# One PSUM tile for each bank in a fused attention and MoE kernel

## The chip, the cores and the metric

The kernel runs on one core of one Trainium2 chip. Its time is the device time of one execution in microseconds; the time shown for a version is the median of several runs. Engines: TensorE (PE, with weight loads as PEld), VectorE (DVE), ScalarE (ACT), GpSimd (POOL) and SyncE (SP), which issues the DMAs. PSUM is the memory that matmuls write: eight banks, each of 512 float32 in each of 128 partitions.

## The reference

```python
def reference(**kwargs):
    ...
    attn_out = _attn_ref(**attn_kwargs)       # q, k, v: 8 x 8 x 576 x 64, softmax in chunks of 64 rows
    B, H, S, D = attn_out.shape
    x = np.ascontiguousarray(attn_out.transpose(0, 2, 1, 3)).reshape(B * S, H * D)   # 4608 x 512
    x = _moe_ref(x=x, **moe_kwargs)           # a = x @ w1; b = x @ w2; ((a * b) @ w3) @ w_out
    return _moe2_ref(x=x, **moe2_kwargs)      # h = x @ w_in; (h * cos(h)) @ w_out
```

w1 and w2 are 512 x 1024, w3 is 1024 x 1024, the first w_out 1024 x 512; w_in is 512 x 2048, the second w_out 2048 x 512. The weights come as 64-bit floats.

## The kernel before

A product of float32 quality is made of float16 halves: each operand is split into a high and a low part, and three matmuls (high x high, high x low, low x high) add up in one bank. That is why matmuls come in threes of lines (L831 to L833, L891 to L893, L1171 to L1173).

The 4608 tokens are nine blocks of 512. The work has these stages:

- Weights (0 to about 200 us, and pieces later): 64-bit words are turned into float32 by DVE, ACT and POOL; w3 and w_out are multiplied into one matrix on PE (`w3_row`: transposes L792, matmuls L800, copies L429).
- Attention (`attention`), 36 tiles of 128 tokens, up to about 760 us: q and k are transposed (L600) into a bank of ps_t and copied (L429); scores (L615) go into a pair of banks; DVE L626 and L629 read the pair; the probabilities are transposed (L649) and copied; the products with v (L664) go into a pair again, which ACT L676 and DVE L679 read.
- `ab`: per block, a and b for eight slices, twelve matmuls each (L831 to L833) into one bank; ACT L857 evicts a, DVE L860 evicts b and multiplies.
- `u_of`: per block four products of 24 matmuls (L891 to L893), evicted by L433 or L435, with scales that pass through small matmuls in ps_t (`all_max`: L461, L469).
- `h_of` and `y_of` (from about 805 us): h is made by seven products (a Strassen form) of six matmuls of 256 columns each (L1101), 42 matmuls a step and eight steps a block, into four banks x, y, z and w; ACT L1116 and DVE L1110 evict them. Then h * cos(h) on ACT, DVE and POOL (L1135 to L1157). y takes 48 matmuls a tile in four pieces of twelve (L1171 to L1173); ACT L1178 evicts a tile, SP L1181 stores it. y of one block runs between steps of h of the next; after the last h only y is left.

The order of the work is not written out by hand. Every step is put down as an operation (`Plan.op`) with its engine, an assumed cost, a due time and the buffers that it reads and writes. `Plan.order` (L110) plays the operations through in assumed time, gives each buffer a place in its pool, and `emit` (L227) writes the instructions in the order found. In each engine's queue the instructions then run in this order. Semaphore waits are not put down by the kernel: the tile framework finds them from the accesses of the instructions to tiles, in the order in which they were written out.

PSUM is four tiles of two banks each (L319, L320): ps_s is banks 0 and 1, ps_t 2 and 3, ps_m 4 and 5, ps_n 6 and 7. The pools hand out banks or pairs of these (L328 to L334):

```python
ps_t = bank_pool(2, 3)                              # transposes, small matmuls
ps_s = pair_pool(0)                                 # attention
ps_s0 = pair_pool(0, 4)                             # attention of the first two blocks
ps_mm = bank_pool(4, 5, 6, 7)                       # w3, ab from block 1 on, u
ps_mm0 = bank_pool(6, 7)                            # ab of block 0
ps_h = bank_pool(0, 1, 2, 3, 4, 5, queue=True)      # h
ps_y = bank_pool(6, 7)                              # y
```

Of the kernel before, what the change touches and what calls it, by code (L numbers as in the profile page):

```python
# [11 lines left out]
F32 = mybir.dt.float32  # L12
# [7 lines left out]
P = 128  # L20
# [13 lines left out]
class Buf:  # L34
# [8 lines left out]

    @property
    def ap(self):
        return self.pool.aps[self.place]


class Pool:
# [11 lines left out]
class Plan:  # L61
# [162 lines left out]
                done += 1  # L224
        return order

    def emit(self):  # L227
        order = self.order()
        for o in order:
            o.fn(o.eng) if o.many else o.fn()  # L230
        return order


PLANS = []
# [3 lines left out]
def fused_kernel(  # L238
# [41 lines left out]
    psum = ctx.enter_context(tc.tile_pool(name="psum", bufs=1, space=bass.MemoryType.PSUM))  # L280
    u_dram = dram.tile([NB, P, KD, T], F32, name="u_dram")

    plan = Plan()
# [23 lines left out]
    def plain(ap):  # L307
        return ap

    def halves_of(ap):  # L310
        return ap.bitcast(F16).rearrange("p (k s e) -> p k s e", s=2, e=512)

    def one_half(ap):
        return ap.bitcast(F16).rearrange("p (s e) -> p s e", s=2)
# [1 line left out]
    def words(ap):  # L316
        return ap.bitcast(U32).rearrange("p (n w) -> p n w", w=2)

    banks = psum.tile([P, 2, 512], F32, name="ps_s"), psum.tile([P, 2, 512], F32, name="ps_t")  # L319
    banks += psum.tile([P, 2, 512], F32, name="ps_m"), psum.tile([P, 2, 512], F32, name="ps_n")  # L320

    def bank_pool(*ix, queue=False):
        return Pool([("PS", i, 1) for i in ix], [banks[i // 2][:, i % 2] for i in ix], queue)

    def pair_pool(*ix):
        return Pool([("PS", i, 2) for i in ix], [banks[i // 2] for i in ix])

    ps_t = bank_pool(2, 3)  # L328
    ps_s = pair_pool(0)
    ps_s0 = pair_pool(0, 4)  # L330
    ps_mm = bank_pool(4, 5, 6, 7)
    ps_mm0 = bank_pool(6, 7)
    ps_h = bank_pool(0, 1, 2, 3, 4, 5, queue=True)
    ps_y = bank_pool(6, 7)  # L334
# [6 lines left out]
        queue=True,  # L341
# [58 lines left out]
    pair = 42 * MM / 2  # L400
# [8 lines left out]
    with tc.manual_schedule():  # L409
# [750 lines left out]
        def y_of(bl):  # L1160
            tg, wout = gh[bl], wpart[1]
            last = bl == NB - 1
            prio = start_h[bl] + (8 * pair + 20.0 if bl == 0 else period) + Y0
            for j in range(TPB):
                ps = Buf(ps_y, f"psy{bl}_{j}")
                for pc in range(4):
                    pr = prio + (pc * 4 + j if last else j * 4 + pc) * 24 * MM
                    def f(ps=ps, j=j, pc=pc):
                        js = slice(j * P, (j + 1) * P)
                        for kk in range(4 * pc, 4 * pc + 4):  # L1170
                            nc.tensor.matmul(ps.ap, tg.ap[:, kk, 0, js], wout.ap[:, kk, 0], start=(kk == 0), stop=False)  # L1171
                            nc.tensor.matmul(ps.ap, tg.ap[:, kk, 0, js], wout.ap[:, kk, 1], start=False, stop=False)  # L1172
                            nc.tensor.matmul(ps.ap, tg.ap[:, kk, 1, js], wout.ap[:, kk, 0], start=False, stop=(kk == K2 - 1))  # L1173
                    ks = range(4 * pc, 4 * pc + 4)
                    op("PE", 12 * MM, pr, f, r=[(tg, (s, kk)) for s in range(2) for kk in ks] + [(wout, kk) for kk in ks], w=[ps])
                yo, iy = Buf(yo_p, f"yo{bl}_{j}"), hsc[bl]
                def f(ps=ps, yo=yo, iy=iy):
                    nc.scalar.activation(yo.ap, ps.ap, AF.Copy, scale=iy[1])  # L1178
                op("ACT", 0.69, pr, f, r=[ps, iy[0]], w=[yo])
                def f(yo=yo, j=j):  # L1180
                    nc.sync.dma_start(out[bl * T + j * P : bl * T + (j + 1) * P, :], yo.ap)  # L1181
                op("SP", 0.6, pr, f, r=[yo], size=P * 2 * KB)
# [28 lines left out]
        for bl in range(NB):  # L1211
# [3 lines left out]
            u_load(bl, start_h[bl] - 12.0)  # L1215
            h_of(bl)
            y_of(bl)
        PLANS.append(plan.emit())


# [28 lines left out]
```

## Time and profile before

| what | value |
|---|---|
| median of 3 runs | 1561.65 us (1561.44 to 1567.07) |
| the profiled execution | 1563.77 us, span 1561.9 us |
| PE busy | 1480.4 us (95%) |
| DVE busy | 1073.8 us (69%) |
| ACT busy | 743.5 us (48%) |
| POOL busy | 376.6 us (24%) |
| mean granted TensorE clock | 0.985 |

Busy is the time in which an engine has an instruction running. A row of a wait names the engine and line that stood idle and, behind the arrow, the tile and line of the instruction that ended the wait. A tile's name covers both of its banks. Matmuls overlap: the next one starts before the last one has ended.

### The profile page before, as it was taken

The numbers are of one execution on the slowest core, as the hardware profiler recorded it, in microseconds if no ns is written. First come the engines' busy times: TensorE is split into PE (matmuls) and PEld (weight loads), VectorE is DVE, ScalarE is ACT, GpSimd is POOL, SyncE is SP. The second block draws the span as 40 slices with busy tenths as digits, with TensorE's granted clock in tenths as the row PEclk, the third lists the DMA queues.
The fourth block names the chain that finished last, engine by engine and source line by source line (L and its number), as shares of the span: only waits on it lengthen the run. The fifth ranks groups of instructions, "written<-read, shape, count | busy, mean of one in ns | idle before, by whom it ended". The sixth has DMA issues, their size and how long they took to land.

```text
span 1561.9 us, 26229 instructions
## 1 busy us (share of the span) xinstructions
PE 1480.4 (95%) x10424; PEld 861.1 (55%) x10424; DVE 1073.8 (69%) x2007; ACT 743.5 (48%) x1206; POOL 376.6 (24%) x295
## 2 busy tenths in 40 slices
PE   6887899999999999999999899999999999999998
PEld 4443444545455545455457566666666666666643
DVE  7867788788664647865458787767777777767610
ACT  5654352465422214512127675656565656556520
POOL 2333224043300101200013343322223222322200
PEclk7999999999999999999999999999999999999999
DMA  9873476757131317380400000010101010100000
GB/s 279 229 182 92 115 256 202 214 170 218 54 89 28 82 28 192 119 264 8 155 35 14 35 15 35 14 41 14 41 15 41 14 42 14 41 14 14 14 21 27
DMA packets 155259, 135.93 MB, mean 87 GB/s; under 512 B 118144, under 2 KB 118144, under 8 KB 153984
## 3 DMA queue, kind: packets, MB, share of 16 engines
q1 hardware_dynamic: 155136, 134.25, 29.0%
q8 instruction: 82, 1.34, 0.4%
q14 instruction: 41, 0.34, 0.1%
HBM read 103.81 MB, written 30.41 MB: 86 GB/s over the span
## 4 chain that ended last, share of the span: by engine, by line
PE 89%; DVE 5%; ACT 4%; issue 1%; DMA 1%; ACTq 0%; SPq 0%; DVEq 0%
PE ps_n L1171 8%; PE ps_n L1172 8%; PE ps_n L1173 8%; PE ps_t L1101 7%; PE ps_s L1101 7%; PE ps_m L1101 7%; PE ps_n L831 4%; PE ps_n L833 4%; PE ps_n L832 4%; PE ps_m L831 4%; PE ps_m L833 4%; PE ps_m L832 4%; PE ps_n L800 3%; PE ps_n L891 2%; PE ps_n L893 2%; PE ps_n L892 2%
## 5 line engine op out<-in xcount | busy, mean ns | idle before, releaser
L1101 PEld LDWEIGHTS <-WIN 128*128 128x128 f16 x3024 | 295.8, 98 | 62.4 <-issue 14.3
L1151 POOL TENSOR_TENSOR WG<-WG,TMP 128x512 f32<-128x512 f32 x119 | 158.8, 1344 | 448.8 <-ACT TMP L1148 428.1
L1101 PE MATMUL ps_t<-XHL,WIN 128*128 128x256 f16 x1032 | 127.2, 273 | 4.2 <-DVE WG L1110 2.5
L1101 PE MATMUL ps_s<-XHL,WIN 128*128 128x256 f16 x1002 | 124.2, 273 | 5.4 <-DVE WG L1110 4.2
L1171 PE MATMUL ps_n<-ATT,W 128*128 128x512 f16 x320 | 122.0, 381 | 4.0 <-ACT TMP L1178 3.2
L831 PE MATMUL ps_n<-XHL,W 128*128 128x512 f16 x308 | 117.3, 381 | 8.8 <-ACT TMP L857 5.8
L1101 PE MATMUL ps_m<-XHL,WIN 128*128 128x256 f16 x990 | 122.9, 273 | 2.1 <-DVE WG L1110 2.0
L1172 PE MATMUL ps_n<-ATT,W 128*128 128x512 f16 x320 | 122.0, 381 | 0.0
L1173 PE MATMUL ps_n<-ATT,W 128*128 128x512 f16 x320 | 121.9, 381 | 0.0
L832 PE MATMUL ps_n<-XHL,W 128*128 128x512 f16 x308 | 117.2, 381 | 0.0
L833 PE MATMUL ps_n<-XHL,W 128*128 128x512 f16 x308 | 117.0, 380 | 0.0
L1135 ACT ACTIVATE TMP<-WG,magic 128x512 f32<-128x512 f32 x144 | 98.9, 711 | 32.3 <-DVE WG L1110 31.8
L1148 ACT ACTIVATE TMP<-TMP,half_pi 128x512 f32<-128x512 f32 x144 | 102.4, 719 | 20.0 <-DVE TMP L1145 17.5
L1139 DVE SCALAR_TENSOR_TENSOR TMP<-TMP,WG 128x512 f32<-128x512 f32 x144 | 106.1, 761 | 1.0 <-ACT TMP L1135 1.0
L831 PE MATMUL ps_m<-XHL,W 128*128 128x512 f16 x268 | 101.6, 379 | 2.5 <-ACT TMP L857 2.5
L644 POOL TENSOR_TENSOR ATT<-ATT,SMALL 128x512 f32<-128x512 f32 x31 | 34.1, 1101 | 287.0 <-DVE SMALL L641 193.7
L833 PE MATMUL ps_m<-XHL,W 128*128 128x512 f16 x268 | 101.6, 379 | 0.0
L832 PE MATMUL ps_m<-XHL,W 128*128 128x512 f16 x268 | 101.6, 379 | 0.0
L1171 PE MATMUL ps_n<-ATT,WG 128*128 128x512 f16 x256 | 97.0, 379 | 2.3 <-ACT TMP L1178 2.3
L832 PEld LDWEIGHTS <-W 128*128 128x128 f16 x576 | 56.4, 98 | 74.0 <-issue 12.4
L1173 PE MATMUL ps_n<-ATT,WG 128*128 128x512 f16 x256 | 97.0, 379 | 0.0
L1172 PE MATMUL ps_n<-ATT,WG 128*128 128x512 f16 x256 | 97.0, 379 | 0.0
(167 smaller groups left out, 2891.9 us busy)
## 6 DMA issues: line engine op xcount, KB each, us to landing
WIN<-in_moe_w_out_dram SPq DMA_DIRECT2D x40, 512.0 KB, 5.1
WIN<-in_moe_w_in_dram SPq DMA_DIRECT2D x32, 512.0 KB, 6.0
ATT<-in_v_dram SPq DMA_DIRECT2D x144, 64.0 KB, 2.5
u_dram<-TMP SPq DMA_DIRECT2D x36, 256.0 KB, 3.6
ATT<-u_dram SPq DMA_DIRECT2D x9, 1024.0 KB, 4.8
out_dram<-TMP SPq DMA_DIRECT2D x36, 256.0 KB, 2.0
ATT<-in_q_dram SPq DMA_DIRECT2D x32, 256.0 KB, 3.8
ATT<-in_k_dram SPq DMA_DIRECT2D x32, 256.0 KB, 4.3
```

Of the source, the lines that this page charges most:

```text
L800: nc.tensor.matmul(acc.ap, wT.ap[:, x * P : (x + 1) * P], wof.ap[:, 0, 4 * g + x], start=(g == 0 and x == 0), stop=(g == 1 and x == 3),)
L831: nc.tensor.matmul(ps, left(kk, 0), right(kk, 0), start=(kk == 0), stop=False)
L832: nc.tensor.matmul(ps, left(kk, 0), right(kk, 1), start=False, stop=False)
L833: nc.tensor.matmul(ps, left(kk, 1), right(kk, 0), start=False, stop=(kk == n - 1))
L1101: nc.tensor.matmul(ps.ap[:, side * half : (side + 1) * half], win.ap[:, b, k, g, w_, fs], t.ap[:, a, k, u_], start=(k == 0 and m == 0), st ...
L1135: nc.scalar.activation(r.ap, hs(), AF.Identity, bias=magic)
L1139: nc.vector.scalar_tensor_tensor(r.ap, r.ap, -MAGIC, hs(), ALU.add, ALU.subtract)
L1148: nc.scalar.activation(r.ap, r.ap, AF.Sin, bias=half_pi, scale=-2.0 * math.pi)
L1151: engines[eng].tensor_tensor(out=hs(), in0=hs(), in1=r.ap, op=ALU.mult)
L1171: nc.tensor.matmul(ps.ap, tg.ap[:, kk, 0, js], wout.ap[:, kk, 0], start=(kk == 0), stop=False)
L1172: nc.tensor.matmul(ps.ap, tg.ap[:, kk, 0, js], wout.ap[:, kk, 1], start=False, stop=False)
L1173: nc.tensor.matmul(ps.ap, tg.ap[:, kk, 1, js], wout.ap[:, kk, 0], start=False, stop=(kk == K2 - 1))
```

## The change

Each bank becomes a tile of its own. Banks 2, 3, 6 and 7 are single tiles from the start. Banks 0 and 1, and 4 and 5, are first one tile of two banks each, in a pool of its own, which attention uses as pairs (other steps may take a half of it in between). `emit` looks up the last operation in the order that uses a pair; after it `split` closes that pair's pool and opens another one in its place, with two single tiles. Buffers look up their bank when an instruction is written out, so that they get whichever tile holds it then.

```diff
@@ class Buf
     @property
     def ap(self):
-        return self.pool.aps[self.place]
+        ap = self.pool.aps[self.place]
+        return ap() if callable(ap) else ap
@@ class Plan
-    def emit(self):
+    def emit(self, split):
+
         order = self.order()
-        for o in order:
+        last = {}
+        for n, o in enumerate(order):
+            for b in o.bufs:
+                if b.pool is not None:
+                    for x in b.pool.places:
+                        if x[0] == "PS" and x[2] == 2 and b.pool.places[b.place] == x:
+                            last[x[1]] = n
+        then = {n: i for i, n in last.items()}
+        for n, o in enumerate(order):
             o.fn(o.eng) if o.many else o.fn()
+            if n in then:
+                split(then[n])
         return order
@@ fused_kernel
-    banks = psum.tile([P, 2, 512], F32, name="ps_s"), psum.tile([P, 2, 512], F32, name="ps_t")
-    banks += psum.tile([P, 2, 512], F32, name="ps_m"), psum.tile([P, 2, 512], F32, name="ps_n")
+
+    banks = {i: psum.tile([P, 512], F32, name=f"ps_{i}") for i in (2, 3, 6, 7)}
+    pairs = {}
+    for i in (0, 4):
+        held = tc.tile_pool(name=f"pair{i}", bufs=1, space=bass.MemoryType.PSUM, side=("left", "right")[i // 4])
+        both = held.__enter__().tile([P, 2, 512], F32, name=f"ps_{i}{i + 1}")
+        pairs[i] = held, both
+        banks[i], banks[i + 1] = both[:, 0], both[:, 1]
+
+    def split(i):
+        pairs.pop(i)[0].__exit__(None, None, None)
+        pool = ctx.enter_context(tc.tile_pool(name=f"single{i}", bufs=1, space=bass.MemoryType.PSUM, side=("left", "right")[i // 4]))
+        banks[i], banks[i + 1] = (pool.tile([P, 512], F32, name=f"ps_{n}") for n in (i, i + 1))

     def bank_pool(*ix, queue=False):
-        return Pool([("PS", i, 1) for i in ix], [banks[i // 2][:, i % 2] for i in ix], queue)
+        return Pool([("PS", i, 1) for i in ix], [lambda i=i: banks[i] for i in ix], queue)

     def pair_pool(*ix):
-        return Pool([("PS", i, 2) for i in ix], [banks[i // 2] for i in ix])
+        return Pool([("PS", i, 2) for i in ix], [lambda i=i: pairs[i][1] for i in ix])
...
-        PLANS.append(plan.emit())
+        PLANS.append(plan.emit(split))
```

## Rows read from the trace of the kernel before

**Rows 1.** The page, the chain that ended last, by engine.

```profile
PE 89%; DVE 5%; ACT 4%; issue 1%; DMA 1%; ACTq 0%; SPq 0%; DVEq 0%
```

**Rows 2.** Busy us of each engine by stage: PE, PEld, DVE, ACT, POOL; granted clock, DMA.

```profile
0.00:200.00 200.00, 158.63 (x1073) 87.10 (x1074) 156.29 (x318) 104.55 (x174) 61.49 (x57) 0.91 0.68 180
200.00:805.00 605.00, 591.53 (x4512) 299.74 (x4510) 412.03 (x927) 218.08 (x351) 113.85 (x92) 1.00 0.44 133
...
870.00:1562.00 692.00, 669.27 (x4395) 430.60 (x4395) 453.60 (x677) 375.36 (x608) 177.99 (x130) 0.99 0.07 25
```

**Rows 3.** Timeline 1490 to 1494.4, PE, then ACT: start us, us, instruction [idle before].

```profile
1490.52 0.38 PE L1171 MATMUL ps_n<-ATT,WG 128*128 128x512 f16 x1
...
1492.89 0.38 PE L1173 MATMUL ps_n<-ATT,WG 128*128 128x512 f16 x1
1494.05 0.38 PE L1171 MATMUL ps_n<-ATT,WG 128*128 128x512 f16 x1 [0.78 <-ACT TMP L1178]
...
1493.31 0.69 ACT L1178 ACTIVATE TMP<-ps_n,smalls 128x512 f32<-128x512 f32 x1 [6.38 <-PE ps_n L1173]
```

**Rows 4.** Timeline 1203 to 1206, PE.

```profile
1203.39 2.13 PE L1101 MATMUL ps_t<-XHL,WIN 128*128 128x256 f16 x18
1205.36 0.38 PE L1171 MATMUL ps_n<-ATT,WG 128*128 128x512 f16 x1
```

**Rows 5.** Timeline 144.5 to 150, DVE, then PE.

```profile
145.04 0.75 DVE L860 SCALAR_TENSOR_TENSOR TMP<-ps_n,smalls,TMP 128x512 f32<-128x512 f32 x1 [3.37 <-PE ps_n L833]
...
145.84 0.38 PE L831 MATMUL ps_n<-XHL,W 128*128 128x512 f16 x1 [0.91 <-DVE TMP L860]
```

**Rows 6.** 870 to 1562: what PE waited for before L1101, then L1171 (us, times).

```profile
  DVE WG L1110: 8.4, 11
  ACT WG L1116: 2.9, 5
...
  ACT TMP L1178: 5.5, 7
```

**Rows 7.** Timeline 964 to 966.5, PE, then DVE.

```profile
965.97 0.70 PE L1101 MATMUL ps_m<-XHL,WIN 128*128 128x256 f16 x5 [1.11 <-DVE WG L1110]
...
965.17 0.75 DVE L1110 SCALAR_TENSOR_TENSOR WG<-ps_m,smalls,WG 128x512 f32<-128x512 f32 x1
```

**Rows 8.** Timeline 1530 to 1562, ACT, its last row.

```profile
1557.71 1.27 ACT L1178 ACTIVATE TMP<-ps_n,smalls 128x512 f32<-128x512 f32 x2 [18.43 <-PE ps_n L1173]
```

**Rows 9.** 200 to 805: PE's waits before L831, into ps_t, and of L615.

```profile
  ACT TMP L857: 6.0, 11
...
  ACT ATT L429: 3.5, 3
...
PE ps_s L615 <- DVE XHL L679: 1.7, 1, 1.7
```

**Rows 10.** 0 to 200: PE's waits before L831, into ps_t; ACT's before L429.

```profile
  DVE TMP L860: 2.9, 4
  ACT TMP L857: 2.3, 3
...
  ACT ATT L429: 6.2, 5
  ACT WIN L429: 4.6, 3
...
  PE ps_m L800: 9.4, 2
```

**Rows 11.** PE at 871.31 (timeline); then busy us and granted clock 873.5 to 877.

```profile
871.31 0.37 PE L461 MATMUL ps_t<-ident,smalls 128*1 128x128 f32 x1 [4.31 <-DVE smalls L458]
...
873.50:877.00 3.50, 3.50 (x9) 1.30 (x10) 3.36 (x10) 2.14 (x4) 2.81 (x2) 0.50 0.01 2
```

**Rows 12.** Banks 4 and 5: DVE's last read as a pair, PE's next write (timelines).

```profile
185.37 0.69 DVE L629 TENSOR_TENSOR ATT<-ps_m,SMALL 128x512 f32<-128x512 f32 x1
...
200.57 0.38 PE L831 MATMUL ps_m<-XHL,W 128*128 128x512 f16 x1
```

## The prediction

> **What bounds the kernel now.** I read the chain that ended last first, then the busy table by stage, then TensorE's waits stage by stage, then short stretches of the timeline. The chain lies on TensorE (PE) for 89% of the span, on VectorE (DVE) for 5% and on ScalarE (ACT) for 4% [rows 1]. So the kernel ends sooner only if PE stands still less. The table by stage says where it stands: 41.4 us of 200 at the start, 13.5 of 605 in the middle, 22.7 of 692 in the last stage. DVE is busy for 78%, 68% and 66% of these stages: it has room in the middle and at the end, and little at the start [rows 2].
>
> The idle time understates a stop. A 512-column matmul is 0.38 us long, but twelve of them start in steps of (1492.89 - 1490.52) / 11 = 0.2155 us, and a stop that shows 0.78 us of idle put the next start 0.94 us late [rows 3]. Each stop costs 0.165 us more than its idle time. For 256 columns it is the same: 18 matmuls take 2.13 us, but what follows starts 1.97 us after them, 0.109 a matmul [rows 4].
>
> **Which stops the change touches.** In the last stage y (L1171 to L1173) has two banks, both in the tile ps_n. ACT evicts a product at 1493.31, after 6.38 us of idling, in the moment in which PE's run of matmuls ends; PE's next matmul into ps_n starts at 1494.05, 0.05 us after that eviction has ended [rows 3]. The twelve matmuls from 1490.52 on and those from 1494.05 on are one product (four pieces of twelve, as y is written out), so its own bank was already in use: PE can only have waited for the read of the other bank. ACT, whose product was complete by 1490.9, can only have waited for writes to the other bank. The two take turns within a tile although the banks differ. In the first block, where a and b have only banks 6 and 7, DVE L860 and PE L831 take turns in the same way [rows 5].
>
> By the Trainium skill, page "PSUM — Partial Sum Buffer", section "PSUM bank collisions raise a hardware error", guarding PSUM by bank is enough; the trace shows it guarded by tile. By that rule all these waits can go and the sum below stands; if a read had to close the whole tile, none could, and the sum would be nothing.
>
> **The parts.** The planner's order, its places and every instruction's size stay; a bank only gets another tile behind it. So nothing is moved past a queue, SP's and POOL's included, and no DMA is added. What changes is which semaphores are waited for, and two exchanges of a pair for two singles are added.
>
> Last stage (870 to 1562). PE idles 8.4 us in 11 stops for DVE L1110, 2.9 in 5 for ACT L1116 and 5.5 in 7 for y's evictions L1178: 16.8 us in 23 stops [rows 6], with 23 x 0.165 = 3.8 us of restarts 20.6. I take those of L1110 and L1116 as waits for another bank too: h takes four of six banks a step, so a bank is written again after a step and a half, and a step is 42 x 0.109 = 4.6 us; yet the wait at 965.97 ends 0.05 us behind an eviction that began only 0.8 us before [rows 7]. At the very end two evictions stand in line, 1.27 us from 1557.71 [rows 8]; the first could be done while PE still writes the other bank, 0.6 us. What is late next is the eviction of the bank itself, some 4 us behind at best, and DVE's queue gets no shorter; I keep 90%: **19 us**, bounds 12 and 21.
>
> Middle (200 to 805). PE L831 idles for ACT L857 6.0 us in 11 stops, 7.8 with restarts. The matmuls into ps_t idle 3.5 us in 3 stops for ACT L429; their two banks are used in turn, so the true reader is often close behind, and I take half, 2. L615's 1.7 us behind DVE L679 is a wait for the pair itself and stays [rows 9]; part of what was gained before it comes back there. I take **8 us**, bounds 4 and 14.
>
> Start (0 to 200). L831's turns with L860 and L857 are 2.9 + 2.3 us in 7 stops, 6.3 with restarts. The matmuls into ps_t idle 6.2 + 4.6 us in 8 stops for ACT L429, 12.1 with restarts. Most of these copies are what the next matmul needs; but ACT is in order, and its copies stand behind others that were held by PE, 9.4 us in two cases [rows 10]. I take half, 6. **12 us**, bounds 0 and 30 (nearly all that PE idles there). It is the least certain term, since DVE's 78% leave it little room.
>
> Between 805 and 870 PE waits 4.31 us for DVE L458 [rows 11], a value of the last u; what PE gains just before is added to that wait, so I count nothing.
>
> The exchanges. The last read of banks 4 and 5 as a pair is DVE L629 at 185.37; the first matmul into that tile after it is at 200.57 [rows 12]. A first write that waits for all that touched the pair is thus covered by 14 us, and that of banks 0 and 1, which attention leaves before h begins, by more. If an exchange stopped all engines instead, it would cost about an eviction and a restart, 1 us each time; I take nothing. More, finer waits: the 18 matmuls at 1203.39 are three groups of six with waits of their own and run without a gap [rows 4], so a wait that is met costs PE nothing; nothing here either.
>
> **Sum.** 19 + 8 + 12 = 39 us. The profiled execution took 1563.77 us (its span is 1561.9), 2.1 more than the median of the three runs, 1561.65. 1563.8 - 39 = 1524.8, and against the median **1523 us**.
>
> **Rivals.** (1) Only the last stage pays: at the start and in the middle DVE and ACT pace the work, and PE just meets the next true wait. For it speaks DVE's 78%; against it that ACT itself idled while L831 waited for it. 1561.65 - 19 = 1543.
>
> (2) The start opens up as a whole, because the turns of ACT and DVE vanish too: 21 + 14 + 30 = 65 us, 1497. Against it: about half of those waits are for data.
>
> (3) The change does nothing: the waits go by bank already, and the stops have another cause. Then 1562. The product that stops after its first piece [rows 3] speaks against it.
>
> (4) Slower, by the clock. If DVE paced the kernel, PE's 39 us of short stops would not vanish but gather into long ones. After the 4.31 us wait at 871 PE ran with a granted clock of 0.50 (the 1.2 GHz level), nine matmuls in 3.5 us [rows 11] where 0.2155 each make 1.9: 1.6 us and more a time. 39 / 4.3 = 9 such waits would add 9 x 1.6 = 15 us and save nothing: 1576. It decides from the point at which DVE is as busy as PE in a stage; with 66% against 97% in the last one it is far from that. The Trainium skill, page "TensorE: Matmul & The Clock Gate", section "What's actually happening", says that throttled is the default and that activity releases the throttle, which is this mechanism; by the same rule stops that are short and do not gather cost nothing more.
>
> **Chances.** Forecast 0.59, (1) 0.16, (2) 0.15, (3) 0.06, (4) 0.04. The first three are faster by over 0.5% (7.8 us, about what a measurement of this kernel can tell from no change): 0.90. No change is (3), 0.06; slower is (4), 0.04. The range goes from the middle of (2) to just past the middle of (1), 1497 to 1547. It takes in the terms' bounds, except nearly all upper or all lower ones at once, and leaves out (3), (4), half of (2) and a little of (1), about 0.2.
>
> **What would show it.** Right: L1171's waits for L1178 and L1101's for L1110 and L1116 gone or under 3 us together; the eviction of a y product begins when its own last matmul ends, not at the end of the other bank's; PE's idle time in the last stage near 5 us; DVE L860 and PE L831 overlapping around 145. Wrong: the same stops again, or as long ones put down to DVE's queue or to data; a lower granted clock in the middle; a stop at the first write after an exchange.

## The result and the profile after

The changed kernel takes **1508.7 us** (median of 4 runs, 1506.63 to 1508.82); the kernel before took 1564.0 us beside it. The ratio is 0.9642, 95% interval 0.9618 to 0.9667: 55.3 us faster. The forecast was 1523 us, 39 us faster, in a range of 1497 to 1547; it was counted from a median of 1561.65, and against that the gain is 53 us. The direction and the mechanism were right; the size was put too low. The profiled execution took 1508.75 us, 55.0 less than the one before.

The page of the changed kernel, busy times and the chain that ended last. Lines of `kernel.py` are 23 higher than before (L1171 is now L1194, L1101 is L1124, L831 is L854), and all PSUM tiles print as `ps`:

```profile
PE 1470.4 (98%) x10424; PEld 859.1 (57%) x10424; DVE 1084.2 (72%) x2007; ACT 744.9 (49%) x1206; POOL 375.4 (25%) x295
...
PE 93%; DVE 3%; ACT 2%; issue 1%; DMA 1%; POOL 0%; SPq 0%; ACTq 0%; DVEq 0%
```

DVE and ACT are busy for about as long as before (1084.2 and 744.9 us, against 1073.8 and 743.5) in a shorter span, and the chain stays on PE for 93% instead of 89% [rows 1]. The changed kernel by stage, cut at the instructions at which [rows 2] is cut (us; busy of PE, PEld, DVE, ACT, POOL; granted clock, DMA):

```profile
0.00:183.00 183.00, 155.72 (x1074) 85.93 (x1074) 156.90 (x315) 103.44 (x174) 60.57 (x57) 0.90 0.75 197
183.00:776.00 593.00, 590.32 (x4511) 299.05 (x4509) 412.11 (x929) 220.10 (x352) 113.60 (x92) 1.00 0.45 135
776.00:838.00 62.00, 60.58 (x447) 43.66 (x446) 50.36 (x88) 45.45 (x75) 23.48 (x17) 1.00 0.10 35
838.00:1507.00 669.00, 663.83 (x4395) 430.42 (x4395) 464.81 (x677) 375.90 (x608) 177.74 (x130) 1.00 0.07 26
```

PE now idles 27.3, 2.7, 1.4 and 5.2 us in the four stages; before it was 41.4 at the start, 13.5 in the middle and 22.7 in the last [rows 2]. All of PE's waits that the trace shows in the last stage of the changed kernel (us in total, times, longest):

```profile
PE ps L484 <- DVE smalls L481: 2.7, 1, 2.7
PE ps L1124 <- DVE XHL L1079: 0.3, 1, 0.3
```

The 23 stops behind evictions [rows 6] are gone, all of them; what is left is the wait for the scale of the last u [rows 11]. The turns themselves, in the changed kernel: PE and ACT in the last stage (timeline: start us, us, instruction, idle before it):

```profile
1440.80 0.38 PE L1196 MATMUL ps<-ATT,WG 128*128 128x512 f16 x1
1441.01 0.38 PE L1194 MATMUL ps<-ATT,WG 128*128 128x512 f16 x1
...
1441.21 0.69 ACT L1201 ACTIVATE TMP<-ps,smalls 128x512 f32<-128x512 f32 x1 [3.94 <-PE ps L1196]
```

A y product ends at 1440.80 + 0.38 = 1441.18; its eviction starts 0.03 us later while PE goes on in the other bank without a stop. In [rows 3] the eviction came only when the other bank's matmuls had ended, and PE stopped for it. The same at the start, for a and b of block 0 [rows 5]:

```profile
141.29 0.38 PE L854 MATMUL ps<-XHL,W 128*128 128x512 f16 x1
...
141.37 0.73 DVE L883 SCALAR_TENSOR_TENSOR TMP<-ps,smalls,TMP 128x512 f32<-128x512 f32 x1
```

DVE reads one bank while PE writes the other. At the very end, ACT's last two rows:

```profile
1500.83 0.69 ACT L1201 ACTIVATE TMP<-ps,smalls 128x512 f32<-128x512 f32 x1 [17.44 <-PE ps L1196]
1503.42 0.69 ACT L1201 ACTIVATE TMP<-ps,smalls 128x512 f32<-128x512 f32 x1 [1.90 <-PE ps L1196]
```

The pair of evictions [rows 8] has come apart: only one, 0.69 us, stands behind the last matmul.

**Where the time came from.** Every engine runs its instructions in the same order in both kernels, so the starts of the same PE instruction can be compared. How much earlier an instruction starts is called the lead here. The changed kernel leads by 17.1 us at 200 us (time of the kernel before), 29.1 at 805, 32.1 at 870 and 54.9 at the end of the span.

| stage | forecast, us | measured, us |
|---|---|---|
| start, 0 to 200 | 12 | 17.1 |
| middle, 200 to 805 | 8 | 12.0 |
| 805 to 870 | 0 | 3.0 |
| last, 870 to 1562 | 19 | 22.8 |
| sum | 39 | 54.9 |

### The profile page after: what moved, and what is told of

Its sections match the earlier page's. It is cut to its first block, busy times and chain, and to the rows that moved or that the text cites. A ratio compares the mean times of both kernels' runs of the same rounds, so it can differ in the third digit from the quotient of the medians.

```text
span 1507.0 us, 26296 instructions
## 1 busy us (share of the span) xinstructions
PE 1470.4 (98%) x10424; PEld 859.1 (57%) x10424; DVE 1084.2 (72%) x2007; ACT 744.9 (49%) x1206; POOL 375.4 (25%) x295
## 4 chain that ended last, share of the span: by engine, by line
PE 93%; DVE 3%; ACT 2%; issue 1%; DMA 1%; POOL 0%; SPq 0%; ACTq 0%; DVEq 0%
PE ps L1124 22%; PE ps L854 8%; PE ps L1196 8%; PE ps L1194 8%; PE ps L1195 8%; PE ps L856 8%; PE ps L855 8%; PE ps L914 4%; PE ps L916 4%; PE ps L915 4%; PE ps L823 3%; PE ps L623 2%; PE ps L687 1%; PE ps L638 1%; PE ps L672 1%
## 5 line engine op out<-in xcount | busy, mean ns | idle before, releaser
L1124 PE MATMUL ps<-XHL,WIN 128*128 128x256 f16 x3024 | 340.0, 273 | 0.3 <-DVE XHL L1079 0.3
L1124 PEld LDWEIGHTS <-WIN 128*128 128x128 f16 x3024 | 295.8, 98 | 46.9 <-issue 0.5
L1133 DVE SCALAR_TENSOR_TENSOR WG<-ps,smalls,WG 128x512 f32<-128x512 f32 (+1 forms) x288 | 193.2, 680 | 82.0 <-PE ps L1124 74.4
L854 PE MATMUL ps<-XHL,W 128*128 128x512 f16 x576 | 219.7, 381 | 1.0 <-ACT TMP L880 1.0
L855 PE MATMUL ps<-XHL,W 128*128 128x512 f16 x576 | 219.3, 381 | 0.0
L856 PE MATMUL ps<-XHL,W 128*128 128x512 f16 x576 | 219.3, 381 | 0.0
L880 ACT ACTIVATE TMP<-ps,smalls 128x512 f32<-128x512 f32 x72 | 49.3, 687 | 159.1 <-PE ps L856 120.3
L1196 PE MATMUL ps<-ATT,W 128*128 128x512 f16 x320 | 122.0, 381 | 0.0
L1194 PE MATMUL ps<-ATT,W 128*128 128x512 f16 x320 | 122.0, 381 | 0.0
L1195 PE MATMUL ps<-ATT,W 128*128 128x512 f16 x320 | 121.9, 381 | 0.0
L883 DVE SCALAR_TENSOR_TENSOR TMP<-ps,smalls,TMP 128x512 f32<-128x512 f32 x72 | 54.0, 749 | 90.7 <-PE ps L856 85.0
L1162 DVE SCALAR_TENSOR_TENSOR TMP<-TMP,WG 128x512 f32<-128x512 f32 x144 | 113.2, 810 | 0.0
L914 PE MATMUL ps<-WG 128*128 128x512 f16 x288 | 109.3, 379 | 0.0
L916 PE MATMUL ps<-WG 128*128 128x512 f16 x288 | 109.2, 379 | 0.0
L915 PE MATMUL ps<-WG 128*128 128x512 f16 x288 | 109.1, 379 | 0.0
L1171 ACT ACTIVATE TMP<-TMP,half_pi 128x512 f32<-128x512 f32 x144 | 102.2, 718 | 9.3 <-DVE TMP L1168 6.8
L1194 PE MATMUL ps<-ATT,WG 128*128 128x512 f16 x256 | 97.0, 379 | 0.0
L1195 PE MATMUL ps<-ATT,WG 128*128 128x512 f16 x256 | 97.0, 379 | 0.0
L1196 PE MATMUL ps<-ATT,WG 128*128 128x512 f16 x256 | 97.0, 379 | 0.0
```

The lines of the kernel that those rows point to most:

```text
L854: nc.tensor.matmul(ps, left(kk, 0), right(kk, 0), start=(kk == 0), stop=False)
L855: nc.tensor.matmul(ps, left(kk, 0), right(kk, 1), start=False, stop=False)
L856: nc.tensor.matmul(ps, left(kk, 1), right(kk, 0), start=False, stop=(kk == n - 1))
L914: nc.tensor.matmul(ps.ap, wh.ap[:, kk, 0, ns], t.ap[:, kk, 0], start=(kk == 0), stop=False)
L915: nc.tensor.matmul(ps.ap, wh.ap[:, kk, 0, ns], t.ap[:, kk, 1], start=False, stop=False)
L916: nc.tensor.matmul(ps.ap, wh.ap[:, kk, 1, ns], t.ap[:, kk, 0], start=False, stop=(kk == K1 - 1))
```

## The experiments

**The theory**: waits go by PSUM tile, so two banks in one tile take turns, and each turn costs PE its idle time and 0.165 us of restart. Rivals: the new places or pools, not the tiles, make the gain; only the last stage pays; the stops move to tiles that are still shared.

**One pair at a time.** All diffs of this group are against the changed kernel. Where a pair is not exchanged, its pool also stays open to the end. Banks 6 and 7 alone:

```diff
-    banks = {i: psum.tile([P, 512], F32, name=f"ps_{i}") for i in (2, 3, 6, 7)}
+    banks = {i: psum.tile([P, 512], F32, name=f"ps_{i}") for i in (2, 3, 6, 7) if i // 2 * 2 not in (2,)}
+    for i in (2,):
+        both = psum.tile([P, 2, 512], F32, name=f"ps_{i}{i + 1}")
+        banks[i], banks[i + 1] = both[:, 0], both[:, 1]
...
     def split(i):
-        pairs.pop(i)[0].__exit__(None, None, None)
...
+        pass
```

> The kernel before with banks 6 and 7 alone as two tiles; banks 2 and 3 are one tile, and the pairs 0/1 and 4/5 stay one tile each to the end. Theory (PE loses its stops, with 0.165 us of restart each, tile by tile): y's turns (5.5 us in 7 stops, so 6.7, and 0.6 at the very end) and those of a and b that lie on ps_n (4.3 us in the middle, 6.3 at the start) go, 18 us together: 1544 against 1562, and TensorE's waits of the first y matmuls for y's eviction are gone, while those of the h matmuls stay (11.3 us in 16 stops). Rival 'only the last stage pays': 7 us. Rival 'DVE paces the first 200 us': 12 us. Rival 'the new places in PSUM, not the tiles': no change, since the banks stay where they are.

Measured: 1535.7 us beside 1562.2; ratio 0.9828 (0.9814 to 0.9843), 26.5 us. PE's waits in the last stage of this kernel:

```profile
PE ps L1125 <- DVE WG L1134: 7.9, 10, 1.1
PE ps L485 <- DVE smalls L482: 4.3, 1, 4.3
PE ps L1125 <- ACT WG L1140: 3.2, 5, 0.9
```

y's waits are gone and those of h stay at 11.1 us in 15 stops. 18 us were expected; most of what came on top lies in the first 200 us. Banks 2 and 3 alone:

```diff
-    banks = {i: psum.tile([P, 512], F32, name=f"ps_{i}") for i in (2, 3, 6, 7)}
+    banks = {i: psum.tile([P, 512], F32, name=f"ps_{i}") for i in (2, 3, 6, 7) if i // 2 * 2 not in (6,)}
+    for i in (6,):
+        both = psum.tile([P, 2, 512], F32, name=f"ps_{i}{i + 1}")
+        banks[i], banks[i + 1] = both[:, 0], both[:, 1]
...
     def split(i):
-        pairs.pop(i)[0].__exit__(None, None, None)
...
+        pass
```

> The kernel before with banks 2 and 3 alone as two tiles; banks 6 and 7 are one tile, and the pairs 0/1 and 4/5 stay one tile each to the end. Theory: the stops of matmuls into ps_t go: 12 us at the start, 3.5 to 4 in the middle, 5.1 of h in the last stage, 21 us together: 1541. My prediction's halves (half of the ps_t stops are for data): 13 us, 1549. Rival 'only the last stage pays': 5 us.

Measured: 1546.8 us; ratio 0.9896 (0.988 to 0.9913), 15.4 us, between the two expected values (21 and 13). PE's waits in the last stage of this kernel:

```profile
PE ps L1125 <- DVE WG L1134: 6.4, 8, 1.1
PE ps L1195 <- ACT TMP L1202: 5.5, 7, 0.8
PE ps L485 <- DVE smalls L482: 4.3, 1, 4.3
PE ps L1125 <- ACT WG L1140: 1.2, 2, 0.6
```

y's seven stops are back to the tenth of a microsecond [rows 6]. The exchanged pairs alone:

```diff
-    banks = {i: psum.tile([P, 512], F32, name=f"ps_{i}") for i in (2, 3, 6, 7)}
+    banks = {i: psum.tile([P, 512], F32, name=f"ps_{i}") for i in (2, 3, 6, 7) if i // 2 * 2 not in (2, 6)}
+    for i in (2, 6):
+        both = psum.tile([P, 2, 512], F32, name=f"ps_{i}{i + 1}")
+        banks[i], banks[i + 1] = both[:, 0], both[:, 1]
```

> The kernel before with only the pairs 0/1 and 4/5 exchanged for single tiles after attention's last use; 2/3 and 6/7 are one tile each. Theory: h's stops in banks 0, 1, 4 and 5 (7.4 us in 9 stops, so 8.9) and those of a and b in 4/5 (3.5 in the middle) go, 12 us together: 1549; nothing changes before 200 us. The three parts (18 + 21 + 12) then add up to 51, near the 55 of the whole change. Rival 'the exchange stops the engines': a stop at the first write after each exchange, 1 to 2 us less. Rival 'the stops move on to the tiles that are still shared': under 5 us here, and the three parts far from adding up.

Measured: 1547.6 us; ratio 0.9907 (0.9892 to 0.9921), 14.6 us, where 12 were expected. In the last stage PE still stops for h's evictions six times, 3.4 us in all, where it did 16 times for 11.3 us [rows 6]; y's seven stops stay. Next, the exchange without the singles:

```diff
...
+    for i in (2, 6):
+        both = psum.tile([P, 2, 512], F32, name=f"ps_{i}{i + 1}")
+        banks[i], banks[i + 1] = both[:, 0], both[:, 1]
...
-        banks[i], banks[i + 1] = (pool.tile([P, 512], F32, name=f"ps_{n}") for n in (i, i + 1))
+        both = pool.tile([P, 2, 512], F32, name=f"ps_again{i}")
+        banks[i], banks[i + 1] = both[:, 0], both[:, 1]
```

> As the run with only the pairs exchanged, but what a pair is exchanged for is again one tile of two banks: the exchange is there, and no bank gets a tile of its own. Theory (waits go by tile): the time of before within 3 us, 1562, with the same stops. Rival 'the exchange itself costs something': 1 to 4 us slower, with a stop at the first write into the new tile. Rival 'the new pools place or order the tiles better': faster by as much as the run with the pairs exchanged for singles.

Measured: 1561.8 us beside 1562.2; ratio 0.9995 (0.9986 to 1.0005). PE's waits in the last stage of this kernel; `ps_again` are the new tiles of two banks:

```profile
PE ps_again L1128 <- DVE WG L1137: 6.2, 7, 1.1
PE ps L1198 <- ACT TMP L1205: 5.5, 7, 0.8
...
PE ps_again L1128 <- ACT WG L1143: 1.2, 2, 0.6
```

The time and the stops of before are back: 7.4 us in 9 stops on the new tiles, as many as on the old ones. So neither the exchange nor the new pools cost or give anything that can be measured. The placement rival falls. Last, banks 2, 3, 6 and 7 as single tiles and no exchange:

```diff
...
     def split(i):
-        pairs.pop(i)[0].__exit__(None, None, None)
-        pool = ctx.enter_context(tc.tile_pool(name=f"single{i}", bufs=1, space=bass.MemoryType.PSUM, side=("left", "right")[i // 4]))
-        banks[i], banks[i + 1] = (pool.tile([P, 512], F32, name=f"ps_{n}") for n in (i, i + 1))
+        pass
```

> The whole change without the exchanges: banks 2, 3, 6 and 7 are tiles of their own, the pairs 0/1 and 4/5 stay one tile each to the end. Theory, with parts that add up: 26.5 (banks 6 and 7 alone) + 15.4 (banks 2 and 3 alone) = 42 us faster, 1520; TensorE's stops in h behind DVE's and ACT's evictions of banks 0, 1, 4 and 5 stay, 7.4 us in 9 stops. What the whole change gains between 805 and 870 us (3.0 us, where the single parts gain 0.5 at most) stays with the pairs, since DVE's evictions of h from them pace the chain to the last u. Rival 'the parts overlap, a stop avoided in one tile comes back in another': 35 us or less, 1527 or more. Rival 'the last 3 us are made by ACT's eviction of u alone': they are gone here too, 45 us.

Measured: 1520.4 us beside 1563.6; ratio 0.9728 (0.9713 to 0.9742), 43.2 us; 42 were expected. The 3.0 us between 805 and 870 came here too, as the last rival said. In the last stage this kernel gains 2.2 us less than the two parts together (11.7 against 8.6 + 5.3, in the table below), so that the sum is met in part by luck. PE's waits in its last stage:

```profile
PE ps L1122 <- DVE WG L1131: 6.7, 8, 1.5
PE ps L482 <- DVE smalls L479: 2.7, 1, 2.7
PE ps L1122 <- ACT WG L1137: 1.2, 2, 0.6
```

The lead over the kernel before by stage, from the starts of the same PE instructions, shows which tile pays where (us):

| run | start | middle | 805 to 870 | last | whole span |
|---|---|---|---|---|---|
| banks 6, 7 | 11.9 | 6.0 | 0.5 | 8.6 | 27.0 |
| banks 2, 3 | 5.9 | 3.9 | 0.4 | 5.3 | 15.5 |
| pairs exchanged | 1.8 | 4.2 | 0.0 | 9.9 | 15.9 |
| pairs rejoined | 1.5 | 0.0 | 0.0 | -0.4 | 1.1 |
| all but the exchange | 17.3 | 9.9 | 3.0 | 11.7 | 41.9 |
| the whole change | 17.1 | 12.0 | 3.0 | 22.8 | 54.9 |

By the medians the three parts give 26.5 + 15.4 + 14.6 = 56.5, the whole 55.3: they add up but for a little. By stage it is less even: in the middle the parts give 6.0 + 3.9 + 4.2 = 14.1, the whole 12.0, since L831's stops at 339.58 and 641.72 (1.0 and 1.1 us) go with either of two changes and are counted twice; between 805 and 870 the parts give 0.9, the whole 3.0. The rival by which stops move on to tiles that are still shared falls, and so does the one that only the last stage pays. Where the pairs are rejoined nothing can be gained, and its 1.5 us at the start show how much two executions differ there by themselves.

**More banks in one tile.** Against the kernel before:

```diff
-    banks += psum.tile([P, 2, 512], F32, name="ps_m"), psum.tile([P, 2, 512], F32, name="ps_n")
+    four = psum.tile([P, 4, 512], F32, name="ps_mn")
+    banks += four[:, 0:2], four[:, 2:4]
```

> The kernel before with banks 4 to 7 as one tile of four banks; the order, the places and the sizes stay. Theory (an eviction waits for the matmuls into any bank of its tile that were written out before it, and the next matmul into the tile waits for that eviction): nearly each product of a and b from block 1 on (128) and of u (36) gets a stop as y's 0.94 us, up to 154 us, less where attention's work comes between; about 100 us slower, 1660 (1610 to 1720), with evictions that begin when the product after theirs ends. Rival 'waits go by bank and the gain came from places or order': 1562 within 5 us.

Measured: 1748.5 us beside 1563.6; ratio 1.1184 (1.1166 to 1.1203), 185 us slower. A turn in the middle of this kernel, PE and then DVE:

```profile
480.47 0.38 PE L832 MATMUL ps_mn<-XHL,W 128*128 128x512 f16 x1 [0.92 <-DVE TMP L861]
...
479.67 0.75 DVE L861 SCALAR_TENSOR_TENSOR TMP<-ps_mn,smalls,TMP 128x512 f32<-128x512 f32 x1 [3.71 <-PE ps_mn L834]
```

And PE's waits over this kernel's whole span, the largest rows:

```profile
PE ps_mn L832 <- DVE TMP L861: 45.3, 48, 2.1
PE ps_mn L832 <- ACT TMP L858: 43.6, 49, 2.9
PE ps_mn L1102 <- DVE WG L1111: 15.5, 18, 2.1
PE ps_s L1102 <- DVE WG L1111: 14.3, 11, 2.4
PE ps_mn L1172 <- DVE WG L1111: 11.2, 12, 2.1
```

97 of the 144 products of a and b now begin with a stop for an eviction, where 18 did before [rows 9, 10], and nothing but the tile was changed. The size was missed. By 870 us of the kernel before this kernel is 132 us behind, within the 154 that were named as the most for a, b and u; the other 53 us come from h and y, which now share a tile with each other and for which nothing had been counted.

**Is there a better version?** The largest waits that are left are for the loads of q and k (8.3 us in 6 stops, all in the first 200 us), for ACT's copies of the weights before L823 (8.3 us in 6 stops, there too; no run was aimed at them) and for the scale of the last u (2.7 us). Six orders of the planner were tried, each by one due time of the changed kernel. For the loads:

```diff
-                op("SP", 0.6, prio - 12, f, w=[b], size=P * 2 * KB)
+                op("SP", 0.6, prio - 20, f, w=[b], size=P * 2 * KB)
```

> The changed kernel with the due time of attention's loads of q and k 8 us earlier (20 instead of 12 before their use); the planner finds its own order from that. TensorE's largest waits that are left are for these loads (8.3 us in 6, so 9.3 with restarts, all in the first 200 us). If they are what bounds the start, 3 to 9 us faster than the changed kernel: 1500 to 1506. If the loads of the weights that are pushed back are as urgent, no change: 1509 within 3 us, with waits for ACT's and DVE's work on the weights in their place.

With `prio - 30`:

> As the run before, 30 instead of 12: the same, or 1 to 3 us better, if the loads bound the start; slower than the changed kernel if three buffers each of q and k fill up and hold the queue of the loads.

With `prio - 9`:

> The changed kernel with the due time of attention's loads of q and k 3 us later (9 instead of 12 before their use), since 8 and 18 us earlier cost 13 and 27 us. If what earlier loads cost is the place that they take in the queue from the loads of the weights, later ones give some of it: 1500 to 1507. If the 8.3 us for which TensorE waits for these loads count in full, it gets worse: 1509 to 1515. If each new order of the planner differs by chance, either.

Measured: 1521.9 us (ratio 0.974, 0.9725 to 0.9755), 1535.8 (0.9824, 0.9809 to 0.9839) and 1508.5 (0.9642, 0.9626 to 0.9658). PE's waits for these loads in the first 220 us, with the loads 8 us earlier:

```profile
PE ps L623 <- DMA ATT<-in_q_dram: 0.6, 1, 0.6
...
PE ps L623 <- DMA ATT<-in_k_dram: 0.5, 1, 0.5
```

The waits for these loads fell from 8.3 to 1.1 us, and the end came 13 us later all the same. Most of the loss lies behind the start: in the first 220 us PE is busy for 191.6 us, against 192.5 in the changed kernel, but between 400 and 780 us it idles 10.7 us instead of 0.3. That stretch in the columns of [rows 2], first the changed kernel, then the one with the loads 8 us earlier:

```profile
400.00:780.00 380.00, 379.74 (x2939) 193.74 (x2938) 230.93 (x553) 112.71 (x179) 40.72 (x33) 1.00 0.34 100
400.00:780.00 380.00, 369.29 (x2859) 189.45 (x2858) 227.56 (x543) 102.49 (x162) 40.13 (x33) 0.98 0.34 100
```

With the loads 18 us earlier PE idles 14.0 us there and is busy for 184.9 us of the first 220. So these two runs price the planner's new order in attention, and say little on whether the loads bound the start; what bounds it was not settled. The first run met neither of its two cases, the second came out slower as one of its cases allowed, but why was not shown. With the loads 3 us later the time is that of the changed kernel, below the losing case and above the gaining one. For the last u, three due times instead of `+ 20.0`:

```diff
-    start_u[NB - 1] = at + 20.0
+    start_u[NB - 1] = at + 12.0
```

> The changed kernel with the due time of the last u 8 us earlier (12 instead of 20 after the first step of h begins). The stop of 2.7 us for the scale of the last u, the largest that is left behind 200 us, and the 3.5 us of matmuls at a granted clock of 0.5 behind it, about 4.5 us together, should be shorter: 1504 to 1507. If h's first block then waits for its evictions instead, no change: 1509 within 3 us. The first 700 us should be as in the changed kernel.

With `+ 24.0`, then `+ 28.0`:

> The changed kernel with the due time of the last u 4 us later (24 instead of 20). With it 8 us earlier the stop for its scale went, but one of 5.3 us for VectorE's halves of the last u came in its place, and the end was 3.4 us later. If more of h stands before that place, both stops shrink: 1503 to 1507. If the scale is then later too by as much, no change: 1509 within 3 us.

> As the run before, 8 us later (28 instead of 20): 1503 to 1507 if h's work covers the stop, since the first block's h then lasts longer than the chain to the scale; 1509 to 1513 if the last u then holds up the first y or the second block.

Measured: 1512.1 us (0.9671, 0.9654 to 0.9687), 1510.8 (0.9666, 0.965 to 0.9681) and 1506.8 (0.9639, 0.9619 to 0.9659). PE's largest waits after 700 us, with `+ 12.0`:

```profile
PE ps L1124 <- DVE XHL L1079: 5.5, 2, 5.3
```

with `+ 24.0`:

```profile
PE ps L484 <- DVE smalls L481: 2.7, 1, 2.7
PE ps L492 <- DVE smalls L487: 2.3, 1, 2.3
```

and with `+ 28.0`:

```profile
PE ps L1194 <- ACT TMP L456: 2.5, 1, 2.5
```

The stop changes its name and stays; 8 us earlier and 4 us later gained nothing. The last version lies within its forecast of 1503 to 1507, but its interval overlaps that of the changed kernel; no version was shown to be faster.

## Why the prediction was right, and where it was too small

**The mechanism** was named as it is: the eviction and the matmul of different banks waited for each other, because they shared a tile. Rejoined pairs and four banks in one tile show it from both sides. What was to show it came: no wait for L1178, L1110 or L1116 is left, y's evictions start with the end of their own product, and PE idles 5.2 us in the last stage where "near 5" was named. In the changed kernel DVE reads one bank at 141.37 while PE writes another. The Trainium skill, page "PSUM — Partial Sum Buffer", section "PSUM bank collisions raise a hardware error", holds a guard by bank to be enough; the trace agrees.

**Last stage, 19 forecast, 22.8 measured.** The stops and their restarts, 20.6 us, and 0.6 at the end make 21.2; the step that failed is "I keep 90%". What was expected to be late next, the eviction of the bank itself, never is: PE has no such wait left. The lead rises by 20.6 us behind the 23 stops, just as counted, and by 0.6 at the end. Another 0.7 us came right behind the wait for the last u's scale: in the 11.69 us from the end of that wait the granted clock is 0.85 in the changed kernel and 0.75 before, where the matmuls at 0.50 [rows 11] went on for longer. By tile the count was close: y 6.7 + 0.6 against 8.6, ps_t's 3.9 us in 7 stops, so 5.1, against 5.3, and the pairs' 8.9 against 9.9.

**Middle, 8 forecast, 12.0 measured.** L831's stops were counted as 7.8 (4.3 on ps_n, 3.5 on ps_m), and that was near: the two runs gave 6.0 and 4.2, of which 2.1 are the same two stops. The steps that failed are the two deductions: half of ps_t's stops (2 counted, 3.9 measured with banks 2 and 3 alone), and the part "that comes back" at L615, which did not: PE's wait there for DVE's read of a pair is 1.0 us in the changed kernel, against 1.7 [rows 9].

**Start, 12 forecast, 17.1 measured.** Half of ps_t's 12.1 us agrees with the 5.9 that banks 2 and 3 alone gave, as far as executions that differ by 1.5 us and more here can tell. L831's turns on ps_n were sized right as well: 6.3 counted, and with banks 6 and 7 alone the lead rises by 6.1 behind these seven stops. But this pair gave 11.9 in all. About 1.5 of it is the granted clock: 0.50 from 105.8 to 109.2 in the kernel before, 1.00 at the same instructions in that run. The step that failed is that L831's own stops were taken for all that the sharing of ps_n costs: the turns also held up ACT and DVE, and stops of PE behind them, some 4 us, were booked as waiting for data. The first, in the kernel before, ACT and then PE:

```profile
95.52 0.59 ACT L429 COPY WIN<-ps_n 128x512 f32<-128x512 f32 x1 [3.84 <-PE ps_n L833]
...
105.48 0.81 PE L792 MATMUL ps_t<-ident,WIN 128*128 128x128 f32 x4 [2.64 <-ACT WIN L429]
```

The same PE instruction with banks 6 and 7 as tiles of their own:

```profile
104.36 0.63 PE L816 MATMUL ps<-ident,WIN 128*128 128x128 f32 x4 [0.82 <-ACT WIN L453]
```

ACT's copy out of one bank idled for the end of L833's matmuls into the other; in that run the same copy comes after 1.10 us for its own L824, and PE's stop behind a later copy is 1.8 us shorter. That the one shortens the other is read from the order of ACT's queue; no run changes it alone. The second goes through DVE. The kernel before, DVE and then PE:

```profile
176.14 0.75 DVE L860 SCALAR_TENSOR_TENSOR TMP<-ps_n,smalls,TMP 128x512 f32<-128x512 f32 x1 [3.46 <-PE ps_n L833]
176.81 0.15 DVE L472 COPY smalls<-ps_t 128x1 f32<-128x1 f32 x1
...
177.01 0.66 PE L600 MATMUL ps_t<-ident,ATT 128*128 128x128 f32 x4 [0.99 <-DVE smalls L472]
```

The same two DVE instructions with banks 6 and 7 as tiles of their own:

```profile
166.19 0.75 DVE L884 SCALAR_TENSOR_TENSOR TMP<-ps,smalls,TMP 128x512 f32<-128x512 f32 x1
167.52 0.16 DVE L496 COPY smalls<-ps 128x1 f32<-128x1 f32 x1 [0.59 <-ACT ATT L453]
```

DVE's eviction no longer idles 3.46 us for the other bank, the copy behind it is in time, and PE's stop of 0.99 us, which looked like a wait for a scale, is gone. Another of 0.65 us behind L679 went in the same way.

**805 to 870, 0 forecast, 3.0 measured.** The step that failed is that what PE gains "is added to that wait": this took the end of the wait as fixed, but the chain to it went through ACT, which took turns too. The kernel before, PE's last matmul of the last u, ACT's eviction of it, and DVE's reduction:

```profile
860.50 0.38 PE L893 MATMUL ps_n<-WG 128*128 128x512 f16 x1
...
863.51 0.69 ACT L433 ACTIVATE TMP<-ps_n,smalls 128x512 f32<-128x512 f32 x1 [0.42 <-PE ps_n L1173]
...
871.10 0.15 DVE L458 TENSOR_REDUCE smalls<-smalls 128x1 f32<-128x4 f32 x1
```

The changed kernel, the same, and PE's wait for that reduction:

```profile
831.02 0.38 PE L916 MATMUL ps<-WG 128*128 128x512 f16 x1
...
839.24 0.27 PE L484 MATMUL ps<-ident,smalls 128*1 128x128 f32 x1 [2.66 <-DVE smalls L481]
...
839.03 0.15 DVE L481 TENSOR_REDUCE smalls<-smalls 128x1 f32<-128x4 f32 x1
...
831.44 0.69 ACT L456 ACTIVATE TMP<-ps,smalls 128x512 f32<-128x512 f32 x1 [1.76 <-PE ps L916]
```

The eviction comes 0.04 us after its product instead of 2.63, the reduction 32.1 us earlier, and the wait [rows 11] falls from 4.31 to 2.66 us. That is 1.65 of the 3.0 us; the rest are a stop of y behind this eviction at 864.25 (0.94) and one of h at 816.34 (0.41), which the forecast held to be lost again in the wait. The wait stayed at 4.3 us with either pair of banks alone and fell to 2.7 with both; the exchange had no part in it, against what was expected of that run. With banks 6 and 7 alone another turn still held the chain:

```profile
836.50 0.75 DVE L1134 SCALAR_TENSOR_TENSOR WG<-ps,smalls,WG 128x512 f32<-128x512 f32 x1 [2.97 <-PE ps L1125]
...
845.09 0.67 ACT L457 ACTIVATE TMP<-ps,smalls 128x512 f32<-128x512 f32 x1
```

DVE idles 2.97 us for h's matmuls (in the kernel before the same instruction idles 2.96 us, and its row names ps_t, which this run leaves shared), and ACT, a few instructions behind DVE's and with no idle time before it, comes to the eviction 2.1 us after the product's end at 842.60 + 0.38.

**The exchanges and the finer waits**, 0 forecast: confirmed by the rejoined pairs. **Rivals**: (1) falls, since the first 805 us gave 29.1 us; (2), 1497, lies nearer to the result than the forecast does, and its mechanism, turns of ACT and DVE that vanish too, had its part at the start and between 805 and 870, but of its 30 us at the start 17.1 came; (3) falls; so does (4): the stops did not gather, and the mean granted clock is 0.986 against 0.985 (its 9 x 1.6 us make 14.4, not 15, which changes nothing).

## What to carry to other kernels

An eviction that starts just when the matmuls of *another* bank end, and a matmul that starts just when the eviction of *another* bank ends, are two banks in one tile: give each bank a tile, and where a pair is needed for a while, exchange it afterwards, which cost nothing here. Price each stop at its idle time and its restart, and take a deduction only for a wait that a row already shows; here the plain sum of the stops was 18.4 + 11.8 + 21.2 = 51 us, the discounted one 39, the truth 55. At the start that sum comes near by luck: of 12.1 counted on ps_t 5.9 came, and stops at one remove made up for it. Where two engines take turns, look also at what stands behind both in their queues: waits that bear the label of data may be turns at one remove.

## What had not been expected

- Sharing costs far more than in proportion: one tile of four banks in place of two tiles of two cost 185 us, where a tile for each bank gave 55.
- The first 200 us differ by some us between executions of the same instructions: 1.5 us in the run with rejoined pairs, and 4.4 us in the one with the last u 8 us later, whose TensorE order is that of the changed kernel up to 839 us. In the latter the granted clock is 0.92 over the first 178.5 us, where the changed kernel has 0.90 over the same instructions. A difference of that size at the start is no result.
- Loads of q and k that came 8 and 18 us earlier removed nearly all waits for them and cost 13 and 27 us, most of the first loss in attention's work between 400 and 780 us.
